# Windowed attention and two MLPs on one NeuronCore: the whole of attention ahead of the first MLP, that MLP on two chunks and then one, another order in the weight stream, and silu as one activation function

## The chip, the cores and the metric

The kernel runs on 1 core of a Trainium2 chip. What counts is the device time of one execution in microseconds (us). The core has four computing engines that run side by side, each through its own list of instructions in order: TensorE (PE, with its weight loads shown as PEld), VectorE (DVE), ScalarE (ACT) and GpSimd (POOL); SyncE (SP) issues nearly all the transfers between memory and the core. They wait for one another by semaphores.

## The reference

Inputs are q, k and v of 2 batches, 8 heads, 768 positions and head size 64. The weights come as doubles and are turned into floats on the chip.

```
keep   = (column < 8) | (0 <= row - column < 96)
scores = q @ k.T / 8 - slope[head] * distance      # only where keep
x = softmax(scores) @ v                            # 1536 tokens x 512
g = x @ w_gate                                     # 512 x 1536
x = (g * (1 / (1 + exp(-g))) * (x @ w_val)) @ w_out
h = x @ w_in                                       # 512 x 2048
out = (h * cos(h)) @ w_out2
```

## The kernel before, in words

**Tiling.** The 1536 tokens are three chunks of 512 (`NCH`, `CT`). Attention works on 12 units, a unit being one chunk and one pair of heads, and each unit is two groups (`NG4` = 24 groups) of two query tiles of 128 rows. A group's tile looks at 128 columns or at 240. `attn_fast` is a generator with these pieces for a group g: `S_` (4 score matmuls on PE, then 4 times on DVE a custom operation that adds the distances and finds the row minimum, and 4 times an exponential on ACT), `R_` (DVE: reciprocals of the sums), `N_` (POOL: 4 multiplications of P by them), `T_` (PE transposes P, ACT copies the result from PSUM to tiles PT), `V_` (PE: P times v; after the second group of a unit `split_out`). `scale` multiplies a unit's q on POOL; `load` issues its q, k and v on SP. A step s runs `T_` of s - LAG, `S_`, `R_` and `N_` of s, `V_` of s - LAG.

**Matmuls of the MLPs.** They are float products made of three passes in a shorter format (`mm3`, lines 370 to 372): each operand is a pair high and low. `split_out` makes the pair of an activation: ACT rounds a copy (line 378), DVE subtracts (line 380). `mlp1` takes a list of chunks: for each of 12 weight units m and each chunk, 24 matmuls (gate in one PSUM bank, value in the next), then silu and the product; then 4 x 36 matmuls per chunk with 6 units of w_out. So MLP 1 has 12 x 24 + 4 x 36 = 432 matmuls of 512 columns per chunk, and `mlp2` has 48 steps of 24. In all, 3 x 432 + 1152 = 2448.

**Weight stream.** Background work that `bg_all` lists: a unit of weights is 128 x 1024. `conv` makes floats of doubles (ACT lines 196 and 212; DVE lines 209, 214, 217, 221), the result is stored to memory and `split_w` makes the pair (ACT line 236, DVE line 238). MLP 1 reads its 18 units twice, the second time from the stored floats. `at` and `bg_fill` place this work among the rest: `at` keeps planned times for each engine, with costs written in the code, and `bg_fill` puts a background operation in where the plan has room. The result is a fixed order on each engine.

**Order of the stages.** `attention_and_first_chunk` runs attention by itself until chunk 0 has its four pairs of heads, and then alternates pieces of attention for chunks 1 and 2 with `mlp1([0])`; in that stretch `mlp1` has two PSUM banks (`banks[6:8]`). Then come `mlp1([1, 2])` with all eight banks, and `mlp2`. The silu is a Tanh on ACT (line 406) and two DVE operations (lines 401 and 412). MLP 1's units stand in 3 buffers w, and two more lie in `t_last`, at first.

Of the kernel before, what the change touches and what calls it, by code (L numbers as in the profile page):

```python
# [27 lines left out]
NPAIR = H // 2  # L28
# [22 lines left out]
GAIN, TMAX, LEAD0, LEAD1 = 1.0, 9.0, 2.5, 2.0  # L51
AHEAD = 30
BG0 = 10
IDLE = 0.2
PTB, PB = 4, 12

NG4, LAG = 24, 2
# [70 lines left out]
class Prologue:  # L128


    def __init__(self, tc, d, st):
# [10 lines left out]
        self.w = [const.tile([128, 2, 1024], F32R, name=f"w{i}") for i in range(3)]  # L142
# [10 lines left out]
class Body:  # L153
# [4 lines left out]
    def weights_setup(self):  # L158
# [5 lines left out]
        self.came, self.bg_ready = {}, 0.0  # L164
# [11 lines left out]
    def load32(self, n):  # L176
        w = self.wr()
        self.nc.sync.dma_start(out=w, in_=self.scr[n])
        self.wf[n] = w
        self.came[n] = self.dma(0.5)  # L180

    def dma(self, size):

        self.t["dma"] = max(self.t["dma"], self.bg_ready) + 2.9 * size
        return self.t["dma"] + 1.5
# [3 lines left out]
    def conv_abs(self, n):  # L189
# [4 lines left out]
        self.bg_ready = max(self.bg_ready, self.came[n])  # L194
        yield "a", 0.97
# [3 lines left out]
    def conv(self, n, ahead=None):  # L199

        v = self.nc.vector
        if n not in self.wa:
            yield from self.conv_abs(n)
        raw, w = self.raw.pop(n), self.wa.pop(n)
        lo, hi = raw[:, :, 0], raw[:, :, 1]
        wi = w.bitcast(I32)
        e = self.se_p.tile([128, 1024], I32, tag="se", name="se")
        yield "d", 0.57
        v.tensor_scalar(out=w, in0=w, scalar1=EXP_LO, scalar2=EXP_HI, op0=ALU.max, op1=ALU.min)  # L209

        yield "a", 0.97
        self.nc.scalar.activation(out=e, in_=lo.bitcast(U32), func=AF.Copy, scale=0.875 * 2.0 ** -29, bias=0.4999)
        yield "d", 0.57
        v.tensor_scalar(out=wi, in0=wi, scalar1=3, scalar2=0x3FFFFFFF,
                        op0=ALU.logical_shift_left, op1=ALU.bitwise_and)
        yield "d", 1.1
        v.scalar_tensor_tensor(out=wi, in0=hi, scalar=-0x40000000, in1=wi, op0=ALU.bitwise_and, op1=ALU.bitwise_or)
        if ahead is not None:
            yield from self.conv_abs(ahead)
        yield "d", 1.1  # L220
        v.tensor_tensor(out=wi, in0=wi, in1=e, op=ALU.bitwise_or)  # L221
        self.wf[n] = w
# [5 lines left out]
    def split_w(self, n, g):  # L228
        w = self.wf.pop(n)
        if g < 2 * (M1 + 6) + 5:  # L230
            hl = self.w_slot(g)
        else:
            hl = self.big_p.tile([128, 2, 1024], F32R, tag=f"big{n}", name=f"big{n}")
        self.bg_ready = max(self.bg_ready, self.came[n])
        yield "a", 0.97
        self.nc.scalar.copy(hl[:, 0], w)  # L236
        yield "d", 1.1
        self.nc.vector.tensor_tensor(out=hl[:, 1], in0=w, in1=hl[:, 0].bitcast(F32), op=ALU.subtract)  # L238
        self.nsplit = g + 1
        self.whl[g] = hl  # L240
        self.wrote["w", g] = (self.bg_ready, "d")

    def w_slot(self, g):

        i = self.slots.index(self.w_last(g))
        self.slots[i] = g
        return (self.pro.w + self.w_more)[i]

    def w_last(self, g):

        N = 2 * (M1 + 6)
        return min(self.slots[3:] if N < g < N + 3 else self.slots[:5 if g < M1 - 4 and self.fast else 3])

    def bg_all(self):
# [3 lines left out]

        def room(g):
            if 2 * N < g < 2 * N + 3:  # L260
                while not self.t_free:
                    yield "wait"
            elif g < 2 * N + 5:

                last = self.w_last(g)
                while last >= 0 and self.big_p is None and self.used <= last + (last >= N + M1):
                    yield "wait"
# [4 lines left out]
        self.load64(0)  # L272
        self.load64(1)
        for n in range(N):
            yield from self.conv(n, n + 1 if n + 1 < N else None)
            self.load64(n + 2)
            self.store32(n)
            yield from room(n)
            yield from self.split_w(n, n)
        nxt = N  # L280
        self.load32(0)
        for n in range(N):
            if n + 1 < N:
                self.load32(n + 1)
            yield from room(N + n)
            yield from self.split_w(n, N + n)
            for _ in range((n + 1) * (N2 - N) // N - n * (N2 - N) // N):
                yield from self.conv(nxt)
                if nxt + 2 < N2:
                    self.load64(nxt + 2)  # L290
                self.store32(nxt)
                del self.wf[nxt]
                nxt += 1
# [3 lines left out]
        for n in range(N, N2):  # L297
            if n + 2 < N2:
                self.load32(n + 2)
            yield from room(N + n)  # L300
            yield from self.split_w(n, N + n)

    def bg_start(self):
        self.used, self.whl, self.wbase, self.converted, self.big_p = -1, {}, 0, False, None
        self.t_free = False
        self.slots = [-5, -2, -1, -4, -3]
# [4 lines left out]
    def bg_step(self, k=1):  # L311

        for _ in range(k):
            if self.bg is None:
                return
            if self.bg_op != "wait":
                e, cost = self.bg_op
                self.ops += 1
                self.bg_ready = self.t[e] = max(self.t[e], self.bg_ready) + cost
# [594 lines left out]
```

## Time and profile before

| | |
|---|---|
| median of 3 runs | 672.81 us (672.36 to 675.93) |
| the profiled execution, its own time | 673.19 us |
| its span, first to last instruction | 671.4 us |
| PE / DVE / ACT / POOL busy share of the span | 95% / 66% / 61% / 11% |
| mean granted TensorE clock | 0.992 |

The span is 1.8 us shorter than the execution's own time. A busy PE counts pipelined matmuls that overlap, so its share says that PE rarely stands idle and nothing on how fast it goes; the start-to-start distances tell that.

### The profile page before, as it was taken

To read this page: it belongs to the slowest core of one execution; us is meant where nothing else is said; L and a number is where in the kernel's file an instruction comes from. 1 tells how busy PE (TensorE), PEld (TensorE's weight loads), DVE (VectorE), ACT (ScalarE), POOL (GpSimd) and SP (SyncE) were. 2 spreads that over 40 slices of the span, in tenths; PEclk is the share of its full clock that TensorE was granted. 3 is DMA by queue.
4 is the path that set the end of the run, shared out by engine and by line. 5 is a ranking of instruction groups with operands and counts; after the bars stand their busy time and mean duration, and the time that the engine had idled before them with its cause. 6 is when DMAs were issued, how large, how long until landed. Compare 5 with 4: busy or idle time off the path is not lost.

```text
span 671.4 us, 8856 instructions
## 1 busy us (share of the span) xinstructions
PE 640.5 (95%) x3176; PEld 514.8 (77%) x3176; DVE 442.3 (66%) x769; ACT 406.7 (61%) x706; POOL 71.0 (11%) x112
## 2 busy tenths in 40 slices
PE   4889999898999999999999999999999999999996
PEld 3556777566777888888888888888888888888885
DVE  3688899888875787877873636876555555554442
ACT  3898778667654545445452427977666556665552
POOL 1563334324200000000000000000000000000000
PEclk9999999899999999999999999999999999999998
DMA  7567556656364654553557062221010000010001
GB/s 275 197 242 240 197 199 241 240 188 232 132 221 164 228 190 186 217 191 126 166 212 246 35 214 68 95 95 62 1 46 18 1 0 1 0 64 1 0 1 67
DMA packets 22660, 88.97 MB, mean 133 GB/s; under 512 B 2640, under 2 KB 3920, under 8 KB 18256
## 3 DMA queue, kind: packets, MB, share of 16 engines
q1 hardware_dynamic: 22176, 88.06, 37.4%
q8 instruction: 27, 0.44, 0.3%
q10 hardware_dynamic: 432, 0.26, 0.1%
q14 instruction: 25, 0.20, 0.1%
HBM read 67.34 MB, written 20.97 MB: 132 GB/s over the span
## 4 chain that ended last, share of the span: by engine, by line
PE 84%; DVE 5%; ACT 5%; issue 2%; DMA 1%; DVEq 1%; POOL 1%; SPq 0%; POOLq 0%; ACTq 0%
PE bank L370 27%; PE bank L372 26%; PE bank L371 26%; PE bank L585 2%; ACT P L601 2%; PE bank L626 2%; PE bank L646 2%; DVE P L598 1%; DMA wr<-scr 1%; ACT w L236 1%; DVE w L238 1%; ACT PT L630 1%; DVE wr L221 1%; ACT wr L196 1%; DVE wr L209 1%
## 5 line engine op out<-in xcount | busy, mean ns | idle before, releaser
L370 PE MATMUL bank<-x,w 128*128 128x512 f32 x304 | 121.1, 398 | 7.3 <-DVE e L401 6.7
L372 PE MATMUL bank<-x,w 128*128 128x512 f32 x304 | 119.1, 392 | 0.5 <-DVE w L238 0.5
L371 PE MATMUL bank<-x,w 128*128 128x512 f32 x304 | 119.0, 391 | 0.0
L465 DVE SCALAR_TENSOR_TENSOR u<-r,bank 128x512 f32<-128x512 f32 x48 | 33.0, 687 | 80.3 <-ACT r L463 80.3
L370 PEld LDWEIGHTS bank<-x,w 128*128 128x128 f32 x304 | 57.2, 188 | 23.3 <-ACT PT L630 3.8
L614 POOL TENSOR_SCALAR P<-P,sum 128x240 f32<-128x240 f32 (+1 forms) x96 | 59.8, 641 | 108.6 <-DVE sum L608 55.2
L372 PEld LDWEIGHTS bank<-x,w 128*128 128x128 f32 x304 | 57.3, 189 | 13.2 <-DVE w L238 1.2
L371 PEld LDWEIGHTS bank<-x,w 128*128 128x128 f32 x304 | 57.2, 188 | 11.2
L601 ACT ACTIVATE P<-P,nmin 128x240 f32<-128x240 f32 (+1 forms) x96 | 45.1, 472 | 26.3 <-DVE nmin L598 26.1
L462 ACT ACTIVATE r<-bank,cst 128x512 f32<-128x512 f32 x48 | 33.0, 688 | 46.0 <-PE bank L372 46.0
L406 ACT ACTIVATE e<-bank 128x512 f32<-128x512 f32 x36 | 21.5, 596 | 61.1 <-PE bank L372 61.1
L238 DVE TENSOR_TENSOR w<-wr,w 128x1024 fp32r<-128x1024 f32 x35 | 43.6, 1246 | 19.4 <-ACT w L236 19.1
L370 PE MATMUL bank<-big,g 128*128 128x512 f32 x144 | 56.0, 389 | 0.0
L371 PE MATMUL bank<-big,g 128*128 128x512 f32 x144 | 56.0, 389 | 0.0
L372 PE MATMUL bank<-big,g 128*128 128x512 f32 x144 | 56.0, 389 | 0.0
L475 DVE TENSOR_TENSOR r<-bank,r 128x512 f32<-128x512 f32 x48 | 33.1, 689 | 28.5 <-ACT r L474 28.5
L473 ACT ACTIVATE r<-r 128x512 f32<-128x512 f32 x48 | 30.4, 633 | 33.7 <-DVE r L466 33.6
L370 PE MATMUL bank<-x,big 128*128 128x512 f32 x120 | 46.7, 389 | 0.0
L371 PE MATMUL bank<-x,big 128*128 128x512 f32 x120 | 46.7, 389 | 0.0
L372 PE MATMUL bank<-x,big 128*128 128x512 f32 x120 | 46.7, 389 | 0.0
L196 ACT ACTIVATE wr<-r 128x1024 f32<-128x1024 f32 x34 | 38.9, 1145 | 12.5 <-DVE w L238 11.6
L236 ACT CAST w<-wr 128x1024 fp32r<-128x1024 f32 x35 | 36.8, 1050 | 13.8 <-DMA wr<-scr 9.2
(107 smaller groups left out, 1336.8 us busy)
## 6 DMA issues: line engine op xcount, KB each, us to landing
scr<-wr SPq DMA_DIRECT2D x34, 512.0 KB, 4.5
wr<-scr SPq DMA_DIRECT2D x34, 512.0 KB, 4.8
r<-in_wo SPq DMA_DIRECT2D x14, 1024.0 KB, 5.3
r<-in_gv SPq DMA_DIRECT2D x12, 1024.0 KB, 5.8
r<-in_win SPq DMA_DIRECT2D x8, 1024.0 KB, 5.8
v<-in_vw SPq DMA_DIRECT2D x11, 512.0 KB, 5.7
out<-wr SPq DMA_DIRECT2D x12, 256.0 KB, 2.4
q<-in_qT SPq DMA_DIRECT2D x7, 256.0 KB, 5.6
```

The source lines that it names most:

```text
L196: self.nc.scalar.activation(out=w, in_=self.raw[n][:, :, 1].bitcast(F32), func=AF.Abs)
L236: self.nc.scalar.copy(hl[:, 0], w)
L238: self.nc.vector.tensor_tensor(out=hl[:, 1], in0=w, in1=hl[:, 0].bitcast(F32), op=ALU.subtract)
L370: mm(out, lhsT=ah, rhs=bh, start=first, stop=False)
L371: mm(out, lhsT=ah, rhs=bl, start=False, stop=False)
L372: mm(out, lhsT=al, rhs=bh, start=False, stop=last)
L462: nc.scalar.activation(out=r, in_=h, func=AF.Identity, scale=INV2PI, bias=self.magic)
L465: nc.vector.scalar_tensor_tensor(out=u, in0=r, scalar=-C1, in1=h, op0=ALU.mult, op1=ALU.add)
L473: nc.scalar.activation(out=r, in_=r, func=AF.Abs)
L475: nc.vector.tensor_tensor(out=r, in0=h, in1=r, op=ALU.mult)
L601: nc.scalar.activation(out=pt[:, :w], in_=pt[:, :w], func=AF.Exp, scale=-1.0, bias=nm, accum_out=sums[g][:, n:n + 1])
L614: nc.gpsimd.tensor_scalar(out=P[g, n][:, :w], in0=P[g, n][:, :w], scalar1=sums[g][:, n:n + 1], scalar2=1.0, op0=ALU.mult, op1=ALU.mult)
```

## The change

- `attention` runs all 24 groups, and only then MLP 1 begins: `mlp1([0, 1])`, then `mlp1([2])`, both with all eight banks.
- A step of `attn_fast` is now: the high half of `split_out` of group s - 4, `T_` of s - 3, `scale`, `S_` of s, `R_` and `N_` of s - 1, the low half of `split_out`, `V_` of s - 3, `load`. `LAG` goes from 2 to 3, the buffers of PT from 4 to 6 and of P from 12 to 20. The copies of PT go to ACT or to DVE, to the one that the plan has free sooner.
- silu is one function on ACT (`AF.Silu`), followed by one DVE product where there were two operations. A dummy Silu stands at the end of attention, and the dummy Sin ahead of MLP 2 is gone.
- The weight stream's `work` interleaves the conversion of a unit n with the making of the pair of another unit m; conversions of MLP 2's units begin among those of MLP 1; the units read from memory again have two buffers of their own (`wl`); w has 4 buffers (`NW`) and the two in `t_last` are gone. The plan's costs and limits have other values.

The core of the diff:

```diff
-BG0 = 10
-IDLE = 0.2
-PTB, PB = 4, 12
-NG4, LAG = 24, 2
+READY = 2.2
+IDLE = 0.5
+PTB, PB = 6, 20
+NG4, LAG = 24, 3
+NW = 4
...
-    def conv(self, n, ahead=None):
+    def work(self, n, ahead, m, g):
...
+        if m is not None:
+            w32, hl = self.wf[m], self.w_buf(m, g)
+            self.bg_ready[m] = max(self.bg_ready.get(m, 0.0), self.came[m])
+            yield "a", 1.05, m
+            self.nc.scalar.copy(hl[:, 0], w32)
...
+        if m is not None:
+            yield "d", 1.24, m
+            v.tensor_tensor(out=hl[:, 1], in0=w32, in1=hl[:, 0].bitcast(F32), op=ALU.subtract)
...
+            if M1 + 6 <= g < 2 * (M1 + 6) - 2:
+                self.load32(m + 2)
...
-                            if g == 1:
-
-                                self.at("d", 0.6, [id(ps[0]), ("s", c, m)], [("s", c, m)])
-                                nc.vector.scalar_tensor_tensor(out=tmp, in0=tmp, scalar=1.0, in1=ps[0],
-                                                               op0=ALU.add, op1=ALU.mult)
                             yield 6
...
-                        nc.scalar.activation(out=tmp, in_=ps[0], func=AF.Tanh, scale=0.5)
+                        nc.scalar.activation(out=tmp, in_=ps[0], func=AF.Silu)
...
-                nc.vector.scalar_tensor_tensor(out=tmp, in0=tmp, scalar=0.5, in1=ps[1], op0=ALU.mult, op1=ALU.mult)
+                nc.vector.tensor_tensor(out=tmp, in0=tmp, in1=ps[1], op=ALU.mult)
...
-                nc.scalar.copy(pt[:nk, :256 * nb], bank[:nk, :256 * nb])
+                e = "a" if self.t["a"] <= self.t["d"] else "d"
+                self.at(e, 0.16 + nb * 0.21, [id(bank)], [("E", g, i)])
+                (nc.scalar.copy if e == "a" else nc.vector.tensor_copy)(pt[:nk, :256 * nb], bank[:nk, :256 * nb])
...
+        for s in range(NG4 + LAG + 1):
             self.wr_free = 3 if s > 1 + LAG else 2 if s > 1 else 0
+            low = X_(s - LAG - 1) if s > LAG else None
+            if LAG <= s < NG4 + LAG:
                 T_(s - LAG)
...
+                if s % 2 == 1 and s // 2 + 1 < len(units):
+                    scale(s // 2 + 1)
                 S_(s)
+
+            if 1 <= s <= NG4:
+                R_(s - 1)
+                N_(s - 1)
+            if low:
+                low()
+            if LAG <= s < NG4 + LAG:
                 V_(s - LAG)
+            if s % 2 == 0 and 0 < s // 2 < len(units) - 1:
+                load(s // 2 + 1)
...
+                for i, chunks in enumerate(([0, 1], [2])):
+                    self.wbase = i * (M1 + 6)
+                    for _ in self.mlp1(chunks, Rot(banks), t_tile):
                         self.bg_fill(self.t["pe"], 4)
```

Where the order moves: PE in the part of the program where chunk 0's MLP 1 used to start. Before (T is line 626, S 585, V 646, MLP 1 is 370 to 372; kk, q, P, PT, v are attention's tiles, x and w MLP 1's):

```order
L585 MATMUL bank_250<-kk,q 128x128
L585 MATMUL bank_251<-kk,q 128x128
L585 MATMUL bank_250<-kk,q 128x240
L585 MATMUL bank_251<-kk,q 128x240
L370 MATMUL bank_256<-x_685,w_78 128x512
L371 MATMUL bank_256<-x_685,w_78 128x512
L372 MATMUL bank_256<-x_685,w_78 128x512
```

Now (T is line 638, S 597, V 660, MLP 1 is 385 to 387), one step of attention, and the end of attention:

```order
L638 MATMUL bank_253<-cst,P 120x128 x4
L638 MATMUL bank_254<-cst,P 120x128 x4
L597 MATMUL bank_258<-kk,q 128x128
L597 MATMUL bank_251<-kk,q 128x128
L597 MATMUL bank_258<-kk,q 128x240
L597 MATMUL bank_251<-kk,q 128x240
L660 MATMUL bank_256<-PT,v 64x128 x8
```

```order
L638 MATMUL bank_254<-cst,P 120x128 x4
L660 MATMUL bank_256<-PT,v 64x128 x8
L385 MATMUL bank_251<-x_503,w_78 128x512
L386 MATMUL bank_251<-x_503,w_78 128x512
L387 MATMUL bank_251<-x_503,w_78 128x512
```

All pieces of attention now stand ahead of the first matmul of MLP 1, in steps of T, S and V, and none stands between its matmuls.

The second place is DVE in attention. Before, with a unit's conversion among it (598 is the custom operation and its short second half, 607 and 608 are `R_` of the same group, 380 `split_out`):

```order
L598 ISA P,nmin<-bank_257,base 128x240
L598 ISA nmin 128x1
L598 ISA P,nmin<-bank_250,base 128x240
L598 ISA nmin 128x1
L217 SCALAR_TENSOR_TENSOR wr_81<-r_322,wr_81 128x1024
L607 TENSOR_SCALAR sum<-sum 128x4
L608 RECIPROCAL sum<-sum 128x4
L380 TENSOR_TENSOR x_580<-bank_255,x_580 128x512
```

Now (610 is the custom operation, 619 and 620 are `R_` of the group before, 400 is `split_out`'s low half, 644 a copy of PT):

```order
L610 ISA P,nmin<-bank_251,base 128x240
L610 ISA nmin 128x1
L619 TENSOR_SCALAR sum<-sum 128x4
L620 RECIPROCAL sum<-sum 128x4
L400 TENSOR_TENSOR x_696<-bank_255,x_696 128x512
L644 COPY PT<-bank_254 120x512
L610 ISA P,nmin<-bank_252,base 128x240
```

DVE gets 36 of the 48 copies of PT (31 of 512 columns, 5 of 256), and ACT keeps 12. Up to the low half of attention's last `split_out`, DVE has 12 operations of the weight stream, 7 of them ahead of the last group's custom operations; ACT has 8 up to the dummy Silu.

## Rows read from the trace of the kernel before

**Rows 1.** The windows view, three stretches; per engine busy us (instructions), clock, DMA share, GB/s
```profile
core 0: us, PE busy (x) PEld busy (x) DVE busy (x) ACT busy (x) POOL busy (x), PEclk, DMA share, GB/s
20.00:40.00 20.00, 15.93 (x155) 11.03 (x155) 14.17 (x57) 19.18 (x58) 12.35 (x23) 1.00 0.61 210
46.00:207.20 161.20, 151.25 (x912) 114.36 (x908) 132.48 (x274) 115.31 (x239) 51.07 (x70) 0.99 0.62 217
207.20:665.10 457.90, 457.35 (x2016) 378.23 (x2016) 282.54 (x377) 258.39 (x369) 0.00 (x0) 1.00 0.26 92
```

**Rows 2.** Timeline of PE, start and end of its work; [idle before <-releaser]
```profile
9.86 2.90 PE L585 MATMUL bank<-wr,wr 64*128 64x128 f32 x16
14.67 1.91 PE L626 MATMUL bank<-cst,P 128*128 128x128 f32 x6 [1.91 <-POOL P L614]
...
207.22 0.50 PE L370 MATMUL bank<-x,w 128*128 128x512 f32 x1 [0.61 <-ACT w L236]
...
664.89 0.39 PE L372 MATMUL bank<-big,g 128*128 128x512 f32 x1
```

**Rows 3.** Timeline of PE in attention: T of group 2; T, S, V, T; T of group 7
```profile
22.45 0.88 PE L626 MATMUL bank<-cst,P 128*128 128x128 f32 x6
...
26.91 1.09 PE L626 MATMUL bank<-cst,P 128*120 128x128 f32 x8
27.93 1.08 PE L585 MATMUL bank<-kk,q 64*128 64x240 f32 x8
28.94 1.09 PE L646 MATMUL bank<-PT,v 120*64 120x128 f32 x16
29.96 0.66 PE L626 MATMUL bank<-cst,P 128*128 128x128 f32 x4
...
43.03 1.09 PE L626 MATMUL bank<-cst,P 128*120 128x128 f32 x8
```

**Rows 4.** Waits of PE from 46 to 200 us: total, times, longest
```profile
PE bank L370 <- DVE e L401: 8.1, 6, 2.8
```

**Rows 5.** Timeline of ACT: an exponential, two copies of PT, a conversion
```profile
19.79 0.48 ACT L601 ACTIVATE P<-P,nmin 128x240 f32<-128x240 f32 x1
20.27 1.04 ACT L630 COPY PT<-bank 120x512 f32<-120x512 f32 x2
21.21 1.21 ACT L196 ACTIVATE wr<-r 128x1024 f32<-128x1024 f32 x1
```

**Rows 6.** Timeline of DVE: custom operations, `R_`, then the subtraction of `split_out`
```profile
30.55 0.39 DVE L598 CUSTOM_DVE_ANT_0 P<-bank,base 128x240 f32<-128x240 f32 x1
30.87 0.40 DVE L598 CUSTOM_DVE_ANT_0 P<-bank,base 128x240 f32<-128x240 f32 x1
...
32.61 0.16 DVE L607 TENSOR_SCALAR sum<-sum 128x4 f32<-128x4 f32 x1
32.90 0.66 DVE L380 TENSOR_TENSOR x<-bank,x 128x512 fp32r<-128x512 f32 x1
```

**Rows 7.** Groups by line on DVE, costliest first: xcount, busy us, mean ns, idle before
```profile
L238 DVE TENSOR_TENSOR w<-wr,w 128x1024 fp32r<-128x1024 f32 x35 | 43.6, 1246 | 19.4 <-ACT w L236 19.1
L217 DVE SCALAR_TENSOR_TENSOR wr<-r,wr 128x1024 int32<-128x1024 int32 x34 | 41.9, 1232 | 0.6
L490 DVE COPY wr<-bank 128x512 f32<-128x512 f32 x6 | 3.9, 684 | 3.0 <-PE bank L372 3.0
```

**Rows 8.** Timeline of POOL: a `scale`, and `N_` at its shortest and its longest
```profile
15.81 0.69 POOL L567 TENSOR_SCALAR q<-q,cst 128x512 f32<-128x512 f32 x1
17.02 1.78 POOL L614 TENSOR_SCALAR P<-P,sum 128x240 f32<-128x240 f32 x4 [0.51 <-DVE sum L608]
...
115.73 4.49 POOL L614 TENSOR_SCALAR P<-P,sum 128x240 f32<-128x240 f32 x4 [4.17 <-DVE sum L608]
```

**Rows 9.** Windows view, columns as in rows 1: two short stretches
```profile
16.00:18.00 2.00, 2.00 (x10) 1.10 (x10) 0.35 (x2) 1.20 (x4) 1.49 (x4) 0.50 1.01 406
120.00:124.00 4.00, 2.69 (x8) 1.69 (x8) 3.50 (x5) 1.63 (x2) 0.22 (x1) 0.69 0.97 381
```

More of the change, by code (lines that the diff above doesn't have):

```diff
@@ L193, in conv_abs @@
         w = self.wr()
-        self.bg_ready = max(self.bg_ready, self.came[n])
-        yield "a", 0.97
+        self.bg_ready[n] = self.came[n]
+        yield "a", 1.12, n
         self.nc.scalar.activation(out=w, in_=self.raw[n][:, :, 1].bitcast(F32), func=AF.Abs)
         self.wa[n] = w
-    def conv(self, n, ahead=None):
+    def work(self, n, ahead, m, g):
         v = self.nc.vector
[L202 to L222, printed above, removed]
@@ L226, in store32, with w_buf @@
         self.dma(0.5)
[L228 to L245, printed above, removed]
+    def w_buf(self, n, g):
+        if g >= 2 * (M1 + 6) + NW:
+            return self.big_p.tile([128, 2, 1024], F32R, tag=f"big{n}", name=f"big{n}")
+        i = self.slots.index(min(self.slots))
         self.slots[i] = g
[L247 to L252, printed above, removed]
+        return self.pro.w[i]
     def bg_all(self):
         N, N2 = M1 + 6, len(self.src)
-        def room(g):
[L260 to L266, printed above, removed]
+        order, nxt = [], N
+        for n in range(N):
+            order.append(n)
+            if n >= 4 and n % 2 == 0:
+                order.append(nxt)
+                nxt += 1
+        order += range(nxt, N2)
+        def room(g):
+            if g < 2 * N + NW:
+                last = min(self.slots)
+                while last >= 0 and self.big_p is None and self.used <= last + (M1 <= last < N):
                     yield "wait"
@@ L270, in room, with work @@
                     yield "wait"
-        self.load64(0)
-        self.load64(1)
-        for n in range(N):
[L275 to L293, printed above, removed]
+        def work(i, m, g):
+            if m is not None:
+                yield from room(g)
+            if i is None:
+                yield from self.work(None, None, m, g)
+                return
+            yield from self.work(order[i], order[i + 1] if i + 1 < N2 else None, m, g)
+            if order[i] >= N:
+                del self.wf[order[i]]
+            if i + 2 < N2:
+                self.load64(order[i + 2])
+        for n in order[:2]:
+            self.load64(n)
+        i = 0
+        for n in range(N + 1):
+            m = n - 1 if n else None
+            while i <= (order.index(n) if n < N else order.index(N - 1)):
+                yield from work(i, m, m)
+                i, m = i + 1, None
+            if m is not None:
+                yield from work(None, m, m)
+        self.load32(0)
+        self.load32(1)
+        left = N2 - i
+        for n in range(N):
+            k = (n + 1) * left // N - n * left // N
+            yield from work(i if k else None, n, N + n)
+            i += k
         self.converted = True
@@ L415, in mlp1 @@
         late.flush()
-        if chunks[-1] == NCH - 1:
-            nc.scalar.activation(out=self.pro.dummy, in_=self.halfpi, func=AF.Sin)
         x2 = {c: [] for c in chunks}
@@ L746, in attn_general, with attention @@
                 self.split_out(xt, banks[4 + k])
-    def attention_and_first_chunk(self, p, banks, t_tile):
-        sc, pv = Rot([banks[i] for i in (0, 1, 6, 7)]), Rot(banks[4:6])
-        at = self.attn_fast(p, sc, Rot(banks[2:4]), pv)
-        for n in at:
-            self.filling, self.goal = n >= BG0, LEAD0 * (n - BG0) / 30
-            if len(self.x[0]) == NPAIR:
-                break
-        sc.items, sc.n = banks[0:2], 0
-        total, n0, n1 = M1 * 24 + KT * 36, n, 4 * (NG4 + LAG) - 1
-        done = 0
-        for cost in self.mlp1([0], Rot(banks[6:8]), t_tile):
-            done += cost
-            self.goal = done / 24 + LEAD0 + (LEAD1 - LEAD0) * done / total
-            while n < n1 and (n - n0) * total < (done + AHEAD) * (n1 - n0):
-                n = next(at)
-        for n in at:
-            pass
+    def attention(self, p, banks):
+        for s in self.attn_fast(p, Rot([banks[i] for i in (0, 1, 6, 7)]), Rot(banks[2:4]), Rot(banks[4:6])):
+            self.filling, self.goal = True, READY * s / NG4
+        self.filling = False
+        self.nc.scalar.activation(out=self.pro.dummy, in_=self.halfpi, func=AF.Silu)
     def run(self):
@@ L807, in run @@
                     if self.fast:
-                        self.attention_and_first_chunk(att_p, banks, t1)
+                        self.attention(att_p, banks)
                     else:
```

130 lines of the change are left out of this document (67 added, 63 removed).

## The prediction

> **What bounds the kernel now.** I read the windows view first, for PE's pace and for the stretch in which attention runs by itself, then the timeline of PE, the waits, and the timelines of ACT, DVE and POOL.
>
> From 207.2 to 665.1 us, which is MLP 1 on chunks 1 and 2 and all of MLP 2, PE runs 2016 matmuls, busy for 457.35 of 457.9 us [rows 1]: 0.2269 us for each, start to start, and 0.55 us of waits. Nothing in this stretch can be had by another order: the engines beside PE are busy for 282.5 and 258.4 us of it. All 2448 matmuls of the MLPs at this pace take 555.4 us.
>
> The rest of the span is attention, its ends and waits. PE's first piece of attention starts at 9.9 us, and the last matmul at 664.9 [rows 2], so from there the tail is 671.4 - 665.1 = 6.3 us. Attention's own work on PE: T, S and V of a wide group follow one another at 26.91, 27.93, 28.94 and 29.96, so 3.05 us for three pieces without a wait [rows 3]. In 8 of the 24 groups one of the two tiles is narrow; there I take 0.2 us less for each piece (T shows 0.88 against 1.09, [rows 3]), so 2.45. Sum: 16 x 3.05 + 8 x 2.45 = 68.4, or 2.85 a group. Then 9.9 + 68.4 + 555.4 + 6.3 = 640.0, and **31.4 us of the span of 671.4 are waits and overheads of PE**.
>
> They lie in two places. (a) Attention by itself, from 9.9 to about 46 us: PE did S of 10 groups, T of 9, V of 8, worth about 25 us, so 11 are lost. The bound there is ACT: from 20 to 40 us it is busy for 19.18 of 20 [rows 1], while PE has 15.93. A group takes 4.1 us (T of group 2 at 22.45, of group 7 at 43.03, so 20.58 for 5 [rows 3]). (b) The mixed stretch, 161.2 us [rows 1] for chunk 0's 432 matmuls (98.0) and the 43 us that attention has left: 20 are lost. Of these, 8.1 are waits on the first silu product, which has to release one of only two banks [rows 4]; most of the rest is what 912 records [rows 1] of alternating kinds lose at each switch, and a fall of the clock (below).
>
> **The change part by part.**
>
> *Mixing goes.* MLP 1 has eight banks for chunk 0 too. The stretch after 207.2, with eight banks, shows 0.55 us of waits in 457.9 [rows 1], so the 8.1 [rows 4] and the switches go. A pair of banks is used again four tiles of 24 matmuls later, 21.8 us, and the operations that must have read it by then take under 1 us each. What replaces (a) and (b) is the pace of 24 steps of attention.
>
> *The pace of a step*, by engine. PE: 2.85, above. ACT: an exponential takes 0.48 from start to start (19.79 to 20.27), a copy of PT 0.47 (two in 20.27 to 21.21) [rows 5]. Four exponentials are 1.92, a copy every second step 0.24, the high half of a split every second step 0.24, and 8 operations of the stream at 1.1 over 24 steps 0.37: 2.8. Before, it was 4 exponentials, two copies (0.94), 0.24 and stream work, which is how it came to 4.1. DVE: a custom operation 0.32 (30.55 to 30.87), `R_` 0.29 (32.61 to 32.90), a split's subtraction 0.66 at most [rows 6]. A copy from PSUM on DVE is in the trace only at 684 ns for 512 columns on a quiet engine [rows 7]; followed by more work it should take 0.6, like the operations of this size that start behind one another, and 0.47 would be the lower end by ACT's. 36 copies in 24 steps at 0.6 are 0.9. So 1.28 + 0.29 + 0.33 + 0.9, and 7 operations of the stream ahead of the last group, 0.65 to 1.25 each [rows 7], 6.5 in 21 steps: 0.3. Sum 3.1. POOL: `N_` 1.78 and half a `scale` of 0.69 [rows 8]: 2.1.
>
> So the work of a step on its fullest engine falls from ACT's 4.1 to DVE's 3.1, with PE at 2.85 right below. The bound moves from ACT to DVE and PE together. ACT reached 96% of its bound from 20 to 40 us [rows 1]; that makes 3.2, and because PE's V waits for DVE's copies of the T before it in the same step, I take another 0.1: **3.3 us a step**. Ends: 2.9, where DVE's copies cost as little as ACT's and PE alone bounds; 4.1, where nothing is gained. I take a value near the lower end because the rows that make it up are all from the stretch that it describes.
>
> *Waits that the new order adds.* `R_` and `N_` come one step later, `T_` one more step after that. In step s - 2 DVE's work up to `R_` of s - 3 ends some 3.4 us after the step began, `N_` 1.8 to 2.0 later; T wants it at 6.6, two steps of 3.3 on, so 1.2 us are to spare. `load` is issued at the end of an even step and not ahead of it; its q waits for the same release as before (the S that read the buffer), and what is queued behind it on SP, the next v and the stream's loads, is needed two steps later or more. On POOL `scale` stands ahead of `N_` as it did. These I cost at nothing.
>
> *Start and end.* The first T was at 14.67 [rows 2]; now `R_` of group 0 comes after the custom operations of group 1, 0.6 later: 15.3. Then 21 full steps of 3.3 are 69.3. The last three steps have no S; from the last S on there follow S and the first custom operation (0.9), four exponentials (1.9), `R_` and `N_` (2.1), T, a copy and V (2.6), 7.5, and five handovers between engines at 0.2: 8.5. Attention ends at 15.3 + 69.3 + 8.5 = **93.1 us**.
>
> *Silu, tables, the weight stream.* One function takes the place of one function on ACT, one DVE product of two goes; PE waited for that product only with two banks. Costed at nothing; the cover is the eight banks. For Silu itself there is no row; anything from a copy (0.47) to a conversion (1.06) would be covered, since ACT has one per 5.4 us. The load of an activation table that came with the dummy Sin comes with the dummy Silu, so one goes and one comes, both on ACT, which PE doesn't wait for there. The stream: a unit of gate and value weights now serves two chunks, 48 matmuls or 10.9 us. DVE then has 1.5 conversions (two operations of 1.23 each and two of little more than half that, so about 4) and one pair, 1.5 x 4 + 1.25 [rows 7], and four operations of its MLP work at 0.7: 10.0. It fits, but not by much, in the first 12 units. With chunk 2 alone a unit has 5.4 us, and DVE half a conversion, a pair and two operations: 4.6. I allow 1.5 us for waits at the three handovers, where [rows 2] shows 0.61 for one.
>
> **Sum.** 93.1 + 555.4 + 6.3 + 1.5 = 656.3 of span, against 671.4 of the profiled execution. Its own time lies 1.8 above its span: **658.1 us**. That execution took 673.19, 0.4 above the median of 672.81; I leave that out.
>
> **Rivals.**
>
> *1. The steps keep the old pace.* Every engine now meets the others three times in a step, and PE and DVE both lack slack. For it: PE waited there too. Against: at 4.1 the bound was ACT's work, of which three quarters of the copies are gone. At 4.1 a step attention ends at 109.9, and the time is 674.9: no change. At 3.7, 666.5.
>
> *2. POOL becomes the bound (slower).* `N_` takes 1.78 at its shortest, but 4.49 where DVE was busiest [rows 8]: the two can hold each other up. DVE now works almost without a break in attention, with 36 copies more. With 4.49 and 0.35 a step would take 4.84, attention end at 125, and the time be 690. It is slower than before by 0.5% from 4.2 a step on, with `N_` at 3.8. Against: the long `N_` stand in the mixed stretch among the stream's long operations, which read two tiles of SBUF; the copies read PSUM. The Trainium skill (SBUF — State Buffer, "SBUF: two separate sides") says the same of the cause: the port pair that VectorE and GpSimd share is locked for a whole instruction, by a VectorE operation in a two-port mode or with two sources in SBUF, and a copy from PSUM is by that neither. The copy at 684 ns for 512 columns [rows 7] agrees that it has no faster mode; that it doesn't lock the pair no row shows.
>
> *3. The clock falls (slower).* From 16 to 18 us, after the pauses of the start, the granted clock is 0.50, and from 120 to 124, about a wait of 2.8 us, 0.69 [rows 9]; from 20 to 40, attention by itself, it is 1.00 [rows 1]. If attention's whole work ran at 1.2 GHz, PE would need 5.7 a step and the time be 708 to 709. It outweighs the gain from 7 of 24 steps on. Against: PE's pauses in a step get shorter than they were from 20 to 40. The Trainium skill (TensorE: Matmul & The Clock Gate, "HAM oscillation — how this bites in real kernels") tells of loops in which PE waits once a turn and loses its clock every turn, which speaks against taking the dense matmuls out from between attention's pieces. The clock of 1.00 from 20 to 40 us [rows 1] doesn't bear it out for this attention.
>
> *4. The stream starves PE in MLP 1.* 10.0 of 10.9 us on DVE; if operations run 15% longer, each of the first 12 units is late by 0.6, and the time 665.
>
> **Chances.** Forecast with its neighbours down to 2.9 a step (650) and up to 3.5, 0.70; rival 4 or a pace between 3.5 and 3.8, still faster, 0.18; rival 1 in full 0.07; rivals 2 and 3 together 0.05. So faster by over 0.5% (below 669.4; about what a measurement can tell) 0.88, within 0.5% 0.07, slower 0.05. The range goes from just under 2.9 a step, 649, to 3.8 a step, 669.
>
> **What would show it.** PE's first matmul of MLP 1 at 93 us; T to T 3.3 us in the steps; DVE the busiest of the engines beside PE there; clock 1.00 from 20 us on; no wait on silu's products; 2448 matmuls in about 557 us. A first matmul of MLP 1 at 110 us makes it wrong; so does a wait for w in MLP 1 of over 5 us in all, or four `N_` at over 3.5 us.

## The result: 665.05 us, faster by 9 us where 15 were forecast

The median of 4 runs is 665.05 us (663.95 to 665.8), that of the kernel before beside them 674.14 (672.36 to 675.93): a ratio of 0.9864, with a 95% interval of 0.9827 to 0.99. That is within the range of the forecast and 7 us above its value. One execution of the kernel that takes chunk 0 alone (below), at 1327.69 us, was in a slow state and is not counted. The profiled execution has a span of 662.6 us, 6.3 more than the sum gave.

The page of the kernel after, first its engines and the clock in 40 slices:

```profile
PE 635.3 (96%) x3176; PEld 517.2 (78%) x3176; DVE 436.8 (66%) x769; ACT 392.7 (59%) x670; POOL 56.7 (9%) x112
...
PEclk9999799999999999999999999999999999999999
```

One slice of the clock stands out, from 66 to 83 us. The windows view answers to [rows 1, 9] (columns as there); all its stretches but the last two lie in attention:

```profile
20.00:40.00 20.00, 18.76 (x198) 14.10 (x198) 18.18 (x80) 16.87 (x59) 15.02 (x32) 1.00 0.62 201
40.00:60.00 20.00, 18.78 (x184) 13.22 (x182) 19.23 (x76) 15.86 (x59) 14.80 (x27) 1.00 0.51 161
67.30:74.00 6.70, 6.67 (x38) 4.97 (x40) 3.04 (x12) 2.49 (x9) 4.19 (x9) 0.55 0.35 134
74.00:80.00 6.00, 5.99 (x64) 4.70 (x64) 5.62 (x24) 4.86 (x18) 2.75 (x7) 1.00 0.52 125
...
100.00:280.00 180.00, 179.86 (x794) 148.53 (x792) 133.40 (x159) 94.04 (x115) 0.00 (x0) 1.00 0.55 193
280.00:656.00 376.00, 372.93 (x1643) 308.24 (x1644) 222.58 (x299) 229.10 (x327) 0.00 (x0) 1.00 0.26 90
```

The bound of attention has moved as forecast: from 20 to 40 us ACT falls from 19.18 to 16.87, PE rises from 15.93 to 18.76, and DVE is the fullest of the others. What went wrong is one place. The timeline of PE (T is line 638, S 597, V 660) from there to the first matmul of MLP 1:

```profile
62.58 0.87 PE L638 MATMUL bank<-cst,P 128*128 128x128 f32 x6
67.33 1.97 PE L597 MATMUL bank<-kk,q 64*128 64x240 f32 x8 [3.88 <-POOL q L579]
69.23 1.55 PE L660 MATMUL bank<-PT,v 128*64 128x128 f32 x12
70.71 1.96 PE L638 MATMUL bank<-cst,P 128*120 128x128 f32 x8
72.60 1.39 PE L597 MATMUL bank<-kk,q 64*128 64x240 f32 x8
...
81.14 1.09 PE L638 MATMUL bank<-cst,P 128*120 128x128 f32 x8
82.16 1.08 PE L597 MATMUL bank<-kk,q 64*128 64x240 f32 x8
83.25 1.09 PE L660 MATMUL bank<-PT,v 120*64 120x128 f32 x16
84.27 1.09 PE L638 MATMUL bank<-cst,P 128*120 128x128 f32 x8
...
97.25 0.50 PE L385 MATMUL bank<-x,w 128*128 128x512 f32 x1
```

From 81.14 to 84.27 a step is T, S, V with no pause, 3.1 us. At 63.5 PE stands for 3.88 us for a scaled q, and then its pieces take nearly twice as long (T 1.89 from start to start, against 1.02), since the granted clock is 0.55, close to the lower level of 1.2 GHz. POOL's `scale` that PE waited for, and SP's queue ahead of it:

```profile
66.56 0.70 POOL L579 TENSOR_SCALAR q<-q,cst 128x512 f32<-128x512 f32 x1 [4.04 <-DMA q<-in_qT]
```

```profile
58.55 0.33 SPq L245 DMA_DIRECT2D scr<-wr  x1
58.98 0.38 SPq L174 DMA_DIRECT2D r<-in_gv  x1
59.46 0.66 SPq L569 DMA_DIRECT2D q<-in_qT  x1
```

SP issues in the order of its list. The store of a converted unit (line 245) stands ahead of q, and it waits for the last DVE operation of that conversion (line 240), which ends at 58.5; SP stands at it for 6.9 us. Behind it come a load of doubles of 1 MB, and q at 59.46, which lands 7 us later.

The waits of PE from attention's start to the end (total, times, longest), those of 0.5 us and more:

```profile
PE bank L597 <- POOL q L579: 3.9, 1, 3.9
PE bank L660 <- DVE PT L644: 3.3, 8, 1.4
PE bank L638 <- POOL P L626: 2.4, 3, 1.3
PE bank L387 <- DVE big L224: 1.8, 1, 1.8
PE bank L597 <- DMA kk<-in_kw: 1.2, 1, 1.2
PE bank L385 <- ACT w L209: 0.9, 1, 0.9
PE bank L387 <- DVE w L224: 0.5, 1, 0.5
```

Behind attention 3.2 us are left: 1.4 for w and 1.8 for MLP 2's first `big`. None is for silu's products.

### The profile page after: what moved, and what is told of

Same layout as the page of the kernel before. It is cut to its first block, busy times and chain, and to the rows that moved or that the text cites. A ratio compares the mean times of both kernels' runs of the same rounds, so it can differ in the third digit from the quotient of the medians.

```text
span 662.6 us, 8727 instructions
## 1 busy us (share of the span) xinstructions
PE 635.3 (96%) x3176; PEld 517.2 (78%) x3176; DVE 436.8 (66%) x769; ACT 392.7 (59%) x670; POOL 56.7 (9%) x112
## 4 chain that ended last, share of the span: by engine, by line
PE 87%; DVE 5%; DMA 3%; ACT 2%; issue 1%; POOL 1%; POOLq 0%; DVEq 0%
PE bank L387 27%; PE bank L385 27%; PE bank L386 27%; PE bank L660 2%; PE bank L597 2%; DMA kk<-in_kw 2%; PE bank L638 2%; DVE P L610 1%; DMA q<-in_qT 1%; DVE PT L644 1%; POOL P L626 0%; DVE x L400 0%; DVE wr L240 0%; DVE w L224 0%; ACT r L475 0%
## 5 line engine op out<-in xcount | busy, mean ns | idle before, releaser
L385 PE MATMUL bank<-x,w 128*128 128x512 f32 x336 | 130.8, 389 | 0.0
L387 PE MATMUL bank<-x,w 128*128 128x512 f32 x336 | 130.7, 389 | 0.0
L386 PE MATMUL bank<-x,w 128*128 128x512 f32 x336 | 130.7, 389 | 0.0
L385 PEld LDWEIGHTS bank<-x,w 128*128 128x128 f32 x336 | 63.1, 188 | 13.2 <-issue 0.2
L387 PEld LDWEIGHTS bank<-x,w 128*128 128x128 f32 x336 | 63.1, 188 | 13.1
L386 PEld LDWEIGHTS bank<-x,w 128*128 128x128 f32 x336 | 63.1, 188 | 13.1
L387 PE MATMUL bank<-x,big 128*128 128x512 f32 x144 | 56.1, 390 | 1.8 <-DVE big L224 1.8
L385 PE MATMUL bank<-t,w 128*128 128x512 f32 x144 | 56.1, 390 | 0.9 <-ACT w L209 0.9
L387 PE MATMUL bank<-t,w 128*128 128x512 f32 x144 | 56.2, 390 | 0.5 <-DVE w L224 0.5
L386 PE MATMUL bank<-t,w 128*128 128x512 f32 x144 | 56.0, 389 | 0.0
L385 PE MATMUL bank<-x,big 128*128 128x512 f32 x144 | 56.0, 389 | 0.0
L386 PE MATMUL bank<-x,big 128*128 128x512 f32 x144 | 56.0, 389 | 0.0
L626 POOL TENSOR_SCALAR P<-P,sum 128x240 f32<-128x240 f32 (+1 forms) x96 | 48.4, 523 | 24.4 <-DVE sum L620 21.8
```

What stands on the lines that cost most here:

```text
L385: mm(out, lhsT=ah, rhs=bh, start=first, stop=False)
L386: mm(out, lhsT=ah, rhs=bl, start=False, stop=False)
L387: mm(out, lhsT=al, rhs=bh, start=False, stop=last)
L626: nc.gpsimd.tensor_scalar(out=P[g, n][:, :w], in0=P[g, n][:, :w], scalar1=sums[g][:, n:n + 1], scalar2=1.0, op0=ALU.mult, op1=ALU.mult)
```

## The experiments

Two questions: what late q cost, and what else MLP 1 stands on. All ratios are to the kernel before, run on the same chip in the same job; its median was between 674.09 and 674.57 us in each, so that times of different jobs can be set side by side to about half a us.

**The store and the next load of doubles behind attention's loads (e1_defer).**

```diff
+    def release(self):
+        held, self.held, keep, self.hold = self.held, [], self.hold, False
+        for fn in held:
+            fn()
...
     def load64(self, n):
+        if self.hold:
+            self.came[n] = self.dma(1.0)
+            self.held.append(lambda: self.load64(n))
+            return
...
                 load(s // 2 + 1)
+            if s > 20 or s % 2 == 0 and s >= 2:
+                self.release()
             yield s
```

> Edit: in attention, the store of a converted unit and the load of the next doubles are issued on SP behind the loads of attention's next unit, not ahead of them; nothing else. Theory A (SP's queue): in the changed kernel q of unit 9 stood on SP behind a store that waited until 58.5 us for DVE, and then shared the transfer engines with that store and 1 MB of doubles; so q goes out at about 57.3 and lands in under 4 us, the 3.9 us wait of PE at 63.4 us goes, and with it the 2.9 us that the lower clock cost from 67 to 74 us. Time 665.05 - 6.8 = 658, range 656 to 660. Theory B (the buffers: q has two, so its load can't start before the S two units earlier, and it is late wherever it stands in the queue): the wait stays at 2 us or more and the time at 663 to 665.

Measured: 664.71 us (663.09 to 666.49), 0.9858 [0.983, 0.9886]; no better than the changed kernel. In attention it does all that was expected. q is issued at 54.51, ahead of the store at 59.01, PE waits 0.2 us for it, the clock stays at 1.00, and MLP 1 begins 5.75 us sooner. The gain is lost in MLP 1. Its windows and its timeline of PE:

```profile
60.00:80.00 20.00, 19.38 (x192) 14.51 (x194) 19.02 (x82) 17.36 (x63) 13.29 (x29) 1.00 0.62 215
220.00:240.00 20.00, 16.99 (x68) 13.16 (x67) 13.89 (x17) 10.19 (x12) 0.00 (x0) 0.91 0.50 181
```

```profile
91.50 0.50 PE L402 MATMUL bank<-x,w 128*128 128x512 f32 x1
...
230.71 0.72 PE L402 MATMUL bank<-t,w 128*128 128x512 f32 x1 [2.90 <-ACT w L222]
```

The waits for w are 4.3 us in all instead of 1.4, and a low clock follows. Theory A was right on attention and wrong on the time: PE got to MLP 1 before the weights did. The edit moves the store and the load of doubles together, so what each of the two cost q was not tried apart.

**All copies of PT on ACT (e2_pt_act).**

```diff
-                e = "a" if self.t["a"] <= self.t["d"] else "d"
+                e = "a"
```

> Edit: all 48 copies of PT on ACT, as before the change; the new steps stay. Theory (the relief of ACT made the steps fast): ACT has 2.8 us a step in the changed kernel and 36 copies at 0.47 over 24 steps more, 3.5; T to T goes from 3.07 to 3.5 us, attention ends about 9 us later, time 674, range 671 to 677. Rival (PE and DVE bound the steps, and the order of R and N alone took the waits out): DVE gets lighter, PE stays at 2.85, time 664 to 666.

Measured: 662.49 us (662.14 to 663.33), 0.9823 [0.9789, 0.9857]: not slower than the changed kernel, as the theory had it, and below the range of the rival too. By the medians it is 2.6 us faster, though the two intervals overlap. ACT is the bound now, without a pause from 40 to 60 us, and PE waits for its copies, but late q is gone and there is no wait for w:

```profile
40.00:60.00 20.00, 16.50 (x176) 12.23 (x174) 13.77 (x66) 20.00 (x64) 13.47 (x28) 1.00 0.77 256
```

```profile
PE bank L660 <- ACT PT L644: 10.2, 12, 1.3
...
PE bank L387 <- DVE big L224: 1.8, 1, 1.8
PE bank L597 <- DMA kk<-in_kw: 1.3, 1, 1.3
PE bank L638 <- POOL P L626: 1.2, 1, 1.2
```

The pace of 3.5 us a step was forecast rightly: from the first T at 14.20 to that of group 21 at 87.66. What the theory left out is that the changed kernel, with its one long wait for q, takes 73.0 us for these 21 steps, and here they take 73.5. The plan also put one unit more of the stream into attention (10 of its DVE operations before attention's last sum, not 7; the expectation of e9_defer_ready below counts one too few in both). That became the next theory: how far the stream is when MLP 1 begins.

**MLP 1 on chunk 0, then on 1 and 2 (e3_chunk0_alone).**

```diff
-                while last >= 0 and self.big_p is None and self.used <= last + (M1 <= last < N):
+                while last >= 0 and self.big_p is None and self.used <= last + (last >= N + M1):
...
-                for i, chunks in enumerate(([0, 1], [2])):
+                for i, chunks in enumerate(([0], [1, 2])):
```

The first line only moves a guard on the buffers w to the pass that now has the two chunks.

> Edit: MLP 1 on chunk 0, then on 1 and 2, as before the change, still all behind attention. Theory (two chunks to a unit are what lets the stream keep up, since conversion now lies behind attention): a unit would be used up in 5.4 us of PE, and DVE needs about 6 for it with its MLP work, and 2 more where a unit of MLP 2 is converted among them; PE waits for w in the first 12 units, 10 to 30 us in all, time 675 to 695. Rival (the stream runs far enough ahead during attention): no change, 664 to 667.

Measured: 739.48 us (738.39 to 739.89), 1.0952 [1.0904, 1.0999]; the direction as expected, the size far more. Waits of PE, and the window of MLP 1 on chunk 0:

```profile
PE bank L385 <- ACT w L209: 56.2, 7, 8.7
```

```profile
95.00:200.00 105.00, 70.70 (x279) 54.70 (x276) 78.80 (x91) 53.85 (x63) 0.00 (x0) 0.83 0.63 219
```

A unit must serve two chunks once attention no longer fills the gaps; with one, PE starves and its clock falls as well.

**The old steps, attention first (e4_old_steps)**: LAG 2, `R_` and `N_` in their own step, PT on ACT.

> Edit: the steps of attention as before the change (lag of 2, R and N in the step of their S, both halves of the split behind V, load ahead, all copies of PT on ACT), with all of attention first and all else as changed. Theory (the steps are worth most of the gain, and taking attention out from between MLP 1's matmuls little by itself): 4.1 us a step as before from 20 to 40 us, attention ends at 110, time 674 to 679. Rival (mixing was the loss): 3.3 us a step or less, time 662 to 668.

Measured: 670.85 us (668.52 to 673.1), 0.9952 [0.9931, 0.9973]. MLP 1 begins at 102.95 us; from the first T at 14.70 to the 23rd at 95.01 a step takes 3.65, not 4.1, and the time lies between the range of the theory and that of the rival. The other edits with the old steps gain 3 us; the new steps are worth 6 to 8 more (665.05 here, 662.49 with the same copies on ACT).

**One unit more of the stream in attention, with the held transfers (e9_defer_ready), and alone (e10_ready).** `READY` is the plan's goal for attention, in units.

```diff
-READY = 2.2
+READY = 3.2
```

> Stores and loads of doubles held back as in e1_defer, and one unit more of the stream converted before attention ends (the goal of the stream in attention 3.2 units instead of 2.2: 9 instead of 6 of its DVE instructions stand before the last sum of attention, as in e2_pt_act). Theory S (what e1_defer saved in attention was given back because the stream was a unit short at the start of MLP 1): the first MLP 1 matmul comes at 92 to 95.5 (91.5 in e1_defer plus up to 4 us for three more DVE instructions of 1.2 us), PE then waits for no w (at most 2 us in all for big and w, against 6.1 in e1_defer), the clock stays at 1.00 in 220 to 240, span 92 to 95.5 + 564.7 (what e2_pt_act took from its first MLP 1 matmul to its end) = 656.7 to 660.2, time 659 to 662. Rival T (the wait at 230 us comes from the order of store and load on SP, or from the clock, and not from how far the stream is at the start): the 2.9 us wait near 230 is there again, and the time is 664 to 667 because attention also got longer.

> One unit more of the stream in attention (goal 3.2 units) as in e9_defer_ready, but with stores and loads where after has them. Theory S (two things are needed: the steps without late q, and the stream a unit ahead): attention ends later by the 4.2 us that the unit cost between e1_defer and e9_defer_ready, first MLP 1 matmul at 99 to 102, no wait for w over 0.5 us, time 664 to 668: no gain on after. Rival T (the unit ahead is what counts, and its work fits beside PE): first MLP 1 matmul at 95 to 97.5, time 660 to 662.5.

Measured together: 659.57 us (657.77 to 661.99), 0.9767 [0.9722, 0.9813]. MLP 1 begins at 95.72, later than in e1_defer by the unit's 4.2 us, and PE waits for no w. Alone: 669.42 us, 0.9932 [0.9904, 0.9961], worse than the changed kernel: q and now kk are late (3.86 at 55.78 and 3.83 at 87.72), and MLP 1 begins at 104.94. So both are needed, as theory S had it, though time and start lie above the ranges it gave. What the traces show of this gain is less than the medians do: e9_defer_ready's profiled execution is the slowest of its four (661.99) and e1_defer's the fastest of its six (663.09), so of the 5.1 us between their medians 1.1 stand in traces. Waits of PE, e9_defer_ready and then e10_ready:

```profile
PE bank L677 <- DVE PT L661: 4.1, 10, 1.0
PE bank L655 <- POOL P L643: 3.1, 5, 1.2
PE bank L404 <- DVE big L237: 1.8, 1, 1.8
PE bank L614 <- POOL q L596: 1.7, 1, 1.7
```

```profile
PE bank L597 <- DMA kk<-in_kw: 5.2, 2, 3.8
PE bank L597 <- POOL q L579: 3.9, 1, 3.9
```

The stream's place can be read from its stores on SP, one for each unit. Set against the first matmul of MLP 1, the third store orders the kernels by their waits for w:

| kernel | MLP 1 begins | third store | store later by | waits for w |
|---|---|---|---|---|
| e1_defer | 91.50 | 99.20 | 7.7 | 4.3 |
| the changed kernel | 97.25 | 101.36 | 4.1 | 1.4 |
| e2_pt_act | 95.68 | 94.97 | -0.7 | 0 |
| e9_defer_ready | 95.72 | 94.50 | -1.2 | 0 |
| e10_ready | 104.94 | 103.72 | -1.2 | 0 |

**PT on ACT and held transfers together (e11_ptact_defer).**

> All copies of PT on ACT (e2_pt_act) and the stores and loads of doubles held back (e1_defer) together. Theory S: in e2_pt_act the steps are bound by ACT (20.00 of 20 us busy in 40 to 60) and PE waits for no q, so the held transfers take nothing away there: first MLP 1 matmul at 95 to 96, no wait for w, 661.5 to 663.5, the same as e2_pt_act's 662.5. Rival T (late q and v cost in e2_pt_act too, hidden in the waits on PT): first MLP 1 matmul at 91 to 93, and the time 658 to 660.

Measured: 662.59 us (661.28 to 663.33), 0.9818 [0.9773, 0.9863], MLP 1 at 95.79: what e2_pt_act has. Where ACT is the bound, the transfers weren't late enough to count.

**The old silu (e5_tanh).**

```diff
+                            if g == 1:
+                                self.at("d", 0.68, [id(ps[0]), ("s", c, m)], [("s", c, m)])
+                                nc.vector.scalar_tensor_tensor(out=tmp, in0=tmp, scalar=1.0, in1=ps[0],
+                                                               op0=ALU.add, op1=ALU.mult)
...
-                        nc.scalar.activation(out=tmp, in_=ps[0], func=AF.Silu)
+                        nc.scalar.activation(out=tmp, in_=ps[0], func=AF.Tanh, scale=0.5)
```

> silu as before the change (Tanh on ACT, and two products on DVE instead of one), the rest as after: one more DVE product of 0.68 us for each of the 36 hidden tiles. Theory A (with eight banks nobody waits for the product, and DVE has room: 15.9 of 20 us busy in 140 to 160): 665 to 666.5, waits of PE on banks under 2 us more than after. Rival B (DVE is what the stream goes by in MLP 1, and 24 products of 0.68 us, 16 us of DVE in 180, put the stream behind): PE waits for w L224 or L209 by 5 to 15 us and the time is 670 to 680.

Measured: 679.26 us (677.4 to 679.75), 1.0063 [1.0039, 1.0087]: with this one part undone, nothing is left of the gain. Rival B was right. The waits of PE, and the windows around the longest:

```profile
PE bank L385 <- ACT w L209: 8.6, 1, 8.6
...
PE bank L387 <- DVE w L224: 3.0, 2, 1.9
```

```profile
238.00:246.00 8.00, 0.48 (x1) 0.48 (x2) 4.04 (x5) 2.90 (x4) 0.00 (x0) 0.64 0.95 353
246.00:254.00 8.00, 7.96 (x26) 5.83 (x26) 7.11 (x9) 4.24 (x5) 0.00 (x0) 0.72 0.51 176
```

No bank is waited for; the stream is late. (The edit also puts back the dummy operations of before, a Tanh and a Sin.) From the third store to the 18th it goes 9.2 us a unit (99.23 to 237.10), in the changed kernel 8.1 (101.36 to 223.00), while DVE has room: 98.78 of 120 us busy from 100 to 220. So it isn't DVE's busy time that sets this pace. What is left is the fixed order, in which a conversion stands among silu operations that wait for PE; that was not tested by itself, and `at` in the edit gives the plan another order as well as DVE another operation.

**One unit at a time in the stream (e16_no_ahead).**

```diff
-            yield from self.work(order[i], order[i + 1] if i + 1 < N2 else None, m, g)
+            yield from self.work(order[i], None, m, g)
```

> The stream converts one unit at a time again (the magnitude of the next unit is no longer taken while the present one is worked on), the rest as after. Theory S (the stream sets the time in MLP 1 as soon as it is slower): each unit's chain then has ACT's 1.15 us, its start and DVE's first step in series, the stream is a unit or more behind by 230, PE waits for w 5 to 15 us in all, time 669 to 680. Rival T (engines have room, 16 and 11 of 20 us busy in MLP 1, and the chain fits anyway): waits for w as in after (3.2 us), time 664 to 667.

Measured: 674.38 us (672.89 to 677.24), 1.0003 [0.9982, 1.0024]: again the whole gain is gone. The stores come 8.8 us apart (101.89 to 233.42 for 15), DVE is busy 86.65 of 120 us from 100 to 220, and PE waits:

```profile
PE bank L387 <- DVE w L224: 5.5, 3, 2.1
...
PE bank L385 <- ACT w L209: 2.1, 1, 2.1
```

In both runs the third store comes 4.1 us after MLP 1's first matmul, as in the changed kernel, so it is the pace that differs and not the start. The stores of the changed kernel show where the pace comes from:

```profile
174.04 0.33 SPq L245 DMA_DIRECT2D scr<-wr  x1
...
190.36 0.33 SPq L245 DMA_DIRECT2D scr<-wr  x1
```

Another store lies between these two, so two conversions take 16.32 us, and three times 24 matmuls of PE at 0.2269 us take 16.34. In the two slower kernels three conversions take 27.2 us for long stretches (127.20 to 154.45 in e5_tanh, 120.16 to 147.36 in e16_no_ahead), which is five times 24 matmuls. So by these traces the order ties the stream to PE's own steps. A run that changes the order alone was not made. From 100 to 220 us ACT stands for PE's result at silu for 24.7 us in the changed kernel, 34.0 in e5_tanh and 35.9 in e16_no_ahead. This also says how near to the edge the changed kernel is: by the order in `bg_all` ten of MLP 1's units need 15 conversions, 121.6 us, and PE uses ten units up in 109. The stream loses 1.3 us a unit to PE and lives on its lead, which is why the table above goes by the lead.

**Two banks for MLP 1 on chunks 0 and 1 (e6_two_banks).**

```diff
-                    for _ in self.mlp1(chunks, Rot(banks), t_tile):
+                    for _ in self.mlp1(chunks, Rot(banks[6:8] if i == 0 else banks), t_tile):
```

> MLP 1 on chunks 0 and 1 with two PSUM banks as in the mixed stretch before, the rest as after. Theory A (the 8.1 us of waits on silu's products before came from having two banks only): with 24 products in the 183 us of this stretch PE waits 8 to 15 us for the reader of a bank, with some lower clock after the waits: 674 to 684. Rival B (they came from engines that were loaded by attention's softmax at the same time, and Silu in one function is done soon enough): waits under 3 us, 665 to 668.

Measured: 666.33 us (664.52 to 666.84), 0.9879 [0.9835, 0.9923], the changed kernel's time within what the intervals can tell, and no wait on a reader of a bank. Two banks alone don't make PE wait. Whether the 8.1 us of [rows 4] went with attention's work beside MLP 1 or with the product of line 401, which released the bank there and has no successor in the changed kernel, wasn't tried apart.

**Towards a better version.** Both start from e9_defer_ready: e13_defer_ready_start also holds back the first two loads of doubles, e14_bias moves more copies of PT to ACT.

```diff
         load(1)
+        self.hold = True
         self.bg_start()
```

```diff
-                e = "a" if self.t["a"] <= self.t["d"] else "d"
+                e = "a" if self.t["a"] <= self.t["d"] + 0.6 else "d"
```

> e9_defer_ready with the first two loads of doubles (1 MB each) issued behind attention's third q, kk and v too, so that kk and q of the first steps come sooner: in e9_defer_ready PE waits 1.7 us for a scaled q near 30, and the clock is 0.91 in 20 to 40. Theory S: that wait and the low clock go, first MLP 1 matmul at 93 to 95, time 657 to 659. Rival T: the doubles come 10 us later, so their conversion lies later in attention and the stream is short again in MLP 1: waits for w of 2 us or more, time 661 to 665.

> e9_defer_ready with fewer copies of PT on DVE (27 instead of 36 of 48), the others on ACT: in e9_defer_ready DVE is busy 19.34 and 19.78 of 20 us in 40 to 80, ACT 15.86 and 17.20. Theory S (DVE is the bound of these steps): PE's 4.1 us of waits on DVE's PT fall under 2, first MLP 1 matmul at 92.5 to 94.5, time 656 to 659. Rival T (ACT's P and sums come late as soon as it carries more, as in e2_pt_act): waits on ACT's PT or on P take their place, 95 to 97, time 659 to 662.

Measured: 658.73 us (658.49 to 660.05), 0.9782 [0.9754, 0.981], and 659.62 us (657.68 to 660.67), 0.9801 [0.9772, 0.983]. MLP 1 begins at 93.23 and 93.11, and neither waits for w. The first is as theory S had it. In the second the waits on DVE's PT fall from 4.1 to 0.7 us, but 2.5 us of waits on ACT's PT take their place, and the time is above theory S's range. They can't be told from e9_defer_ready or from each other, but the first's interval, like that of e9_defer_ready, lies wholly below that of the changed kernel. What PE still waits for in e13_defer_ready_start:

```profile
PE bank L677 <- DVE PT L661: 4.4, 11, 1.0
PE bank L655 <- POOL P L643: 3.1, 5, 1.3
PE bank L404 <- DVE big L237: 1.8, 1, 1.8
```

Both edits in one kernel weren't tried.

## Why the prediction was right, and where it was off

*The pace of a step: right, a little too slow.* 21 steps were put at 3.3 us. The first T comes at 14.89, the T of group 21 at 87.87: 73.0 for 21. Of that, 3.9 is the wait for q, 1.2 a wait for kk, and 2.7 the low clock behind the first (four pieces from 67.33 to 73.92 take 6.6 us; at full clock 3.9). The other 65.2 are 3.1 a step. The terms held: DVE's copy of PT takes 0.6 from start to start (50.12 to 50.72), as was put, and DVE is the fullest engine beside PE.

*"These I cost at nothing": the step that failed.* The prediction held that what is queued behind `load` on SP is needed two steps later. It asked what `load` holds up, and not what holds `load` up: a store that waits for DVE, and 1 MB ahead of q. That is 3.9 + 2.7 = 6.6 us of attention. e1_defer shows it for the two together, with MLP 1 5.75 us sooner once the transfers change places.

*The ends.* From the T of group 21 to MLP 1 it took 9.4 us, not 8.5; the start was 0.4 early. One cause of the 0.9 can be seen: attention's last `N_` instruction takes 1.96 us (from 93.36) instead of 0.47, and PE waits 0.65 for it. In all 97.25 against 93.1: 3.7 from the steps, 0.9 from the end, less 0.4.

*The MLPs: right.* From 97.25 to 656.3 (the last matmul starts at 656.19) are 559.05 us, less 3.2 of waits 555.8, where 555.4 was forecast. The waits were put at 1.5. Together, 4.15 + 0.4 + 1.7 = 6.25 of the 6.3 that the span was off.

*Silu and the stream: the second failure, hidden in the sum.* "Costed at nothing; the cover is the eight banks." The old silu costs 14.2 us in this arrangement (679.26 against 665.05), and not by a bank: the stream gets slower. "It fits, but not by much" looked at DVE's busy time, 10.0 of 10.9 us a unit; that isn't what decides, since in e16_no_ahead DVE is less busy and the stream later. Even in the changed kernel a unit's 1.5 conversions take 12.2 us, not 10.9: it doesn't fit, and the lead covers it. That the sum came out near is partly luck: it had no term for the lead or for the pace, and the change as made has just enough of both. The parts can't be added up: undone singly, the old steps, the old silu and the single unit cost 5.8, 14.2 and 9.3, while all of the change gains 9. Silu and the pairing keep MLP 1 from starving, and without either the time won in attention is lost there.

*The rivals.* Rival 1 fell with the steps, and even the old steps took 3.65 and not 4.1. Rival 2 fell: the longest `N_` is 3.34 us (four instructions at 56.38), the mean of one 523 ns, and in the groups by line POOL waits for DVE's sums and hardly for anything else:

```profile
L626 POOL TENSOR_SCALAR P<-P,sum 128x240 f32<-128x240 f32 (+1 forms) x96 | 48.4, 523 | 24.4 <-DVE sum L620 21.8 <-ACT P L613 2.6
```

Where `N_` is long, an operation of the stream with two tiles of SBUF stands beside it: an instruction that takes 0.46 us at 92.48, beside a copy of PT (92.05 to 92.74), takes 1.43 at 90.62, beside the stream's at 90.51 (1.21 us), and 1.96 at 93.36, beside the one at 93.25 (1.22 us) and the next. The longest group, at 56.38, has the stream's operation of 57.30 beside it. The Trainium skill (SBUF — State Buffer, "SBUF: two separate sides") names as what locks the shared port pair a VectorE operation in a two-port mode or with two inputs in SBUF. The trace agrees with that for the stream's operations, and that a copy from PSUM doesn't lock the pair is what the 0.46 us show. Rival 3 fell for the steps (clock 1.00 from 20 to 60) but came once, after one long wait. The Trainium skill (TensorE: Matmul & The Clock Gate, "HAM oscillation — how this bites in real kernels") has the lower clock follow waits for transfers; 0.55 after 3.88 us without q agrees, and the pauses between attention's pieces don't bring it here. Rival 4 is at the door: 1.4 us in the changed kernel, 4.3 as soon as attention gets faster, 56.2 with one chunk.

## What to carry to other kernels

Where one engine issues loads, read its queue from the late load backwards: a store that waits for compute holds up every load behind it, however early their buffers are free. When a stage is shortened, look at what the next stage consumes, and how far its producer is when it starts: here the 5.75 us won in attention showed in the time only after one more unit was converted there, which itself cost 4.2. A producer on in-order engines is not safe because those engines show idle time: its pace can be tied to the consumer's by the order of the instructions. Put its progress (its stores) beside the consumer's.

## What the runs showed of the hardware

In these runs the price of a low clock is paid mostly after the wait. In the changed kernel the granted clock was still 0.89 while PE stood (63.5 to 67.3), and 0.55 in the 6.7 us of work after that:

```profile
63.50:67.30 3.80, 0.00 (x0) 0.00 (x0) 1.54 (x4) 1.49 (x7) 0.74 (x2) 0.89 1.01 396
```

In e1_defer a wait of 2.9 us was followed by 0.73 from 231 to 237, while after the 1.24 us wait for kk at 20.6 the changed kernel had 1.00. A GpSimd multiplication of 0.46 us took 1.43 and 1.96 us beside VectorE operations that read two tiles of SBUF, and kept its 0.46 beside a copy from PSUM (times above). Silu, for which no row of before stood, takes 597 ns for 512 columns, between the bounds of 0.47 and 1.06 us that were set.
